# Turning the solved blocks behind the second gap's mixture pieces, from the sixth unit on

## The chip, the cores and the metric

The kernel runs on one core of one Trainium2 chip. The core has a matrix engine (TensorE, "PE" in the profile, with its weight loads as "PEld"), three engines for elementwise work (VectorE "DVE", ScalarE "ACT", GpSimd "POOL"), a queue that issues transfers (SyncE "SP"), the on-chip memory SBUF and the accumulators of TensorE, PSUM. The metric is the time on the device in microseconds (us), the median of the runs of a version.

## The reference

Two blocks follow each other. The first is a recurrence over 768 time steps for 4 batches of 8 heads of size 40, the second a mixture of four small networks whose weights are given by normalised probabilities:

```python
# r, k, v, w, a, b: (4, 8, 768, 40)
for t in range(S):
    kt, vt, rt = (k[:, :, t], v[:, :, t], r[:, :, t])
    wt, at, bt = (w[:, :, t], a[:, :, t], b[:, :, t])
    y[:, :, t] = np.einsum('bhd,bhde->bhe', rt, state)
    Sa = np.einsum('bhde,bhe->bhd', state, at)
    state_decay = state * wt[:, :, None, :] - np.einsum('bhd,bhe->bhde', Sa, bt)
    state = state_decay + np.einsum('bhd,bhe->bhde', vt, kt)
# y as x: (3072, 320)
p = domain_probs / (domain_probs.sum(-1, keepdims=True) + 1e-09)
for e in range(4):                            # w1: (4, 320, 1024), w2: (4, 1024, 320)
    h = np.maximum(x @ w1[e], 0.0)
    out += p[:, e:e + 1] * (h @ w2[e])
```

All of it is computed in fp32.

## The kernel before

The recurrence is cut into 12 chunks of 64 steps. A **unit** is one chunk of two batches, so there are 24 units, u = 0 to 23. For a unit the kernel does the following, and each part is a generator that is run up to its next `yield` by calls of `run`:

- `within`: the parts that don't need the state (G is the running product of w, then the turned copies NT, KT, AT, RT, VT, and products of them).
- `substitute`: a triangular system of 32 x 32 blocks is solved, on GpSimd for the units that matter here, step by step into Z. It takes about 22 us.
- `merge`: the solved blocks are turned (Qc, then QTc, on VectorE), copied to QT by GpSimd, and joined to 64 x 64 blocks by products pY and pQ on TensorE.
- `step`: the state goes one chunk on.

The mixture of a chunk runs beside the recurrence of the next units. It is cut into pieces in a list `todo`: `ups` (x @ w1 into ph, clipped by ScalarE into hs), `down_1` and `down_2` (products into PSUM tiles p, which VectorE adds, scaled by the gate, to the output tile osb). `gap(n)` of the main loop takes pieces off this list.

```python
    def merge(q):                                             # first stage
        Qc = sb.tile([P, H, Q], FP32, name="Qc", tag="q", bufs=2)
        QTc = sb.tile([P, H, Q], FP32, name="QTc", tag="q", bufs=2)
        tc.keep_in_program_order(nc.vector.transpose(out=dealt(Qc[:]), in_=q.Z))            # L568
        tc.keep_in_program_order(nc.vector.transpose(
            out=QTc[:].rearrange("p h r -> p (h r)"), in_=Qc[:].rearrange("p h c -> p (h c)")))   # L570
        q.QT = QTs()
        for i in range(P // Q):
            ins = nc.gpsimd.tensor_copy(out=q.QT[quarter(i), :, quarter(i % 2)], in_=QTc[quarter(i)])  # L576
            tc.keep_in_program_order(ins)
        yield
        py = big("pY")                                        # second stage
        for h in range(H):
            for i in (1, 3):
                nc.tensor.matmul(out=py[quarter(i - 1), h * Q:(h + 1) * Q], lhsT=q.F[quarter(i), h, 0:Q],
                                 rhs=QTc[quarter(i), h, :], start=True, stop=True)          # L583
        ...   # Yq copied from pY by ScalarE; yield; pQ (L595) from Qc and Yq, copied into QT (L600)
```

```python
    def add(to, p, sc, start=False):
        if start:
            nc.vector.tensor_scalar(out=to, in0=p, scalar1=sc, scalar2=None, op0=ALU.mult)               # L750
        else:
            nc.vector.scalar_tensor_tensor(out=to, in0=p, scalar=sc, in1=to, op0=ALU.mult, op1=ALU.add)  # L752
    ...
        def products(name, *terms):
            p = ps.tile([P, len(terms) * HD], FP32, name=name, tag="mm", bufs=3)
            ...   # matmuls, L841
        def down_1(e):
            p = products("p431", ...)
            ...
            for q, o in zip(qs, osb):
                add(o[:], p[:, wide], scale(q, e), e == 0)
            for q, o, cols in zip(qs, osb, (left, right)):
                add(o[:, cols], p[:, DM:DM + HD], scale(q, e))
```

The main loop, one pass for each u from 1 on (m is `merge` of unit u + 1, w is `within` of unit u + 2, s is `step`, `early` is u < 5):

```python
        run(w_next); run(s, 1); gap(0)
        early = u < 5
        if early:
            run(s, 1)
        run(w, 1)
        run(s)
        ...   # the chunk's mixture pieces are put on the list
        run(w, 1)
        if not early:
            run(m, 1)          # first stage of merge
        gap(1)
        ...   # loads of unit u + 3
        run(w, 2)
        if early:
            run(m, 1)
        else:
            run(s_next, 1)
            run(m, 1)          # second stage: pY
        gap(2)
        ...   # rest of merge, of within and of step; substitute(u + 2); gap(3)
```

A scheduler orders the recorded instructions of each engine; those given to `keep_in_program_order` keep their place among each other.

Of the kernel before, what the change touches and what calls it, by code (L numbers as in the profile page):

```python
# [15 lines left out]
def kernel(  # L16
# [154 lines left out]
    def begin(u):  # L171
        q = Unit()
        q.u, q.c, q.bp = u, u // (B // 2), u % (B // 2)
        q.b = [2 * q.bp, 2 * q.bp + 1]
        q.start, q.end = q.c == 0, q.c == NC - 1
        q.n = {}
        units.append(q)
        return q

    def load(q, names):  # L180
        for x in names:
            q.n[x] = t = sb.tile([P, H, D], FP32, name=f"nat{x}", tag=f"nat{x}", bufs=2 if x in "WV" else 1)
            for i, bb in enumerate(q.b):
                nc.sync.dma_start(
                    out=t[i * L:(i + 1) * L], in_=srcs[x][bb, :, q.c * L:(q.c + 1) * L, :].rearrange("h t e -> t h e"),
                )

    def load_raw(q, names):


        moves = []
        for x in names:
            q.n["raw" + x] = t = raw[x]()
            heads = srcs[x].rearrange("b h t e -> (b h) t e")[q.b[0] * H:(q.b[1] + 1) * H, q.c * L:(q.c + 1) * L, :]
            heads = heads.rearrange("n (x two) e -> x n (two e)", two=2)
            for r in range(2):
                if x in "RV":

                    sets = ((slice(0, 8, 2), slice(r, 16, 4)), (slice(1, 8, 2), slice(3 - r, 16, 4)))
                else:  # L200
                    sets = ((slice(0, 8), slice(r, 16, 2)),)
                for n, hs in sets:
                    for y, w_ in enumerate((D + Q, 2 * D - Q)):
                        o = slice(64 * r + Q * y, 64 * r + Q * y + Q)
                        moves.append(lambda eng, out=t[o, n, 0:w_], in_=heads[:, hs, Q * y:Q * y + w_]: eng.dma_start(out=out, in_=in_))
        return moves
# [10 lines left out]
    def go(moves, eng=None):  # L217
        for move in moves:
            move(eng or nc.sync)
# [343 lines left out]
    def merge(q):  # L563
# [5 lines that stand above are left out]
        tc.keep_in_program_order(  # L569
            nc.vector.transpose(  # L570
                out=QTc[:].rearrange("p h r -> p (h r)"), in_=Qc[:].rearrange("p h c -> p (h c)"),
# [8 lines that stand above are left out]
        py = big("pY")  # L580
        for h in range(H):
            for i in (1, 3):
                nc.tensor.matmul(  # L583
                    out=py[quarter(i - 1), h * Q:(h + 1) * Q], lhsT=q.F[quarter(i), h, 0:Q],
                    rhs=QTc[quarter(i), h, :], start=True, stop=True,
                )
        Y = sb.tile([P, H, Q], FP32, name="Yq")
        for i in (0, 2):
            nc.scalar.copy(out=Y[quarter(i)].rearrange("p h t -> p (h t)"), in_=py[quarter(i), 0:H * Q])
        yield  # L590

        pq = big("pQ")
        for h in range(H):
            for i in (0, 2):
                nc.tensor.matmul(  # L595
                    out=pq[quarter(i), h * Q:(h + 1) * Q], lhsT=Qc[quarter(i), h, :],
                    rhs=Y[quarter(i), h, :], start=True, stop=True,
                )
        for i in (0, 2):
            nc.scalar.copy(out=q.QT[quarter(i), :, quarter(1)], in_=by(pq[quarter(i), 0:H * Q], Q))  # L600
        yield
# [160 lines left out]
    def mixture_of_unit(q):  # L762

        hs, at = {}, 2 * E * q.u

        def ups(e):
            hs[e] = [up(at + 2 * e + x, q.xT, P, P) for x in range(2)]
            used(at + 2 * e + 2)
            if q.u == 0 and e + 2 < E:
                load_w2(e + 2)  # L770

        def down(e):
            po = ps.tile([P, DM], FP32, name="po", tag="mm", bufs=3)
            for f in range(NF):
                nc.tensor.matmul(  # L775
                    out=po[:], lhsT=hs[e][f // HF][:, f % HF, 0:P], rhs=w2_sb[e][:, f, :],
                    start=(f == 0), stop=(f == NF - 1),
                )
            if e == 0:
                q.osb = outputs()  # L780
            add(q.osb[:], po[:], scale(q, e), e == 0)
            if e == E - 1:
                store(q, q.osb)

        todo.append(lambda: ups(0))
        for e in range(E):
            todo.append(lambda e=e: down(e))
            if e + 1 < E:
                todo.append(lambda e=e: ups(e + 1))
# [113 lines left out]
    def begin_later(n):  # L903
        for move in later[:n]:
            tc.keep_in_program_order(move(nc.sync))
        del later[:n]

    def mix(n):

        for piece in todo[:n]:  # L910
            piece()
            begin_later(3 if n > 1 else 6)
        del todo[:n]

    def run(gen, n=99):
        if gen is None:
            return
        for _ in range(n):
            if next(gen, gen) is gen:
                break  # L920
# [3 lines left out]
    def begin_step(u):  # L924
        q = units[u]
        if q.bp == 0:
            chunks_x[q.c] = sb.tile([P, 3, 2 * P], FP32, name="xT", tag="xT", bufs=2)
        q.xT = chunks_x[q.c][:, :, q.bp * P:(q.bp + 1) * P]
        return step(q, q.xT)
# [91 lines left out]
    for u in range(1, NU):  # L1021
        q = units[u]
        m = s_next = w = w_next = iter(())
        if u + 1 < NU:
            m, s_next = merge(units[u + 1]), begin_step(u + 1)
            w_next = ws[u + 1]
        if u + 2 < NU:
            w = ws[u + 2]

        def gap(n, pieces=None):  # L1030
            at = 4 * u + n
            run(sum_ops, sums_at.get(at, 0))
            mix((1 if at in sparse else 2) if pieces is None else pieces)

        run(w_next)
        run(s, 1)
        gap(0)
# [7 lines that stand above are left out]
        if u == 1:  # L1045
            mixture_of_unit(q)
        elif q.bp:
            mixture_of_chunk(units[u - 1:u + 1], chunks_x[q.c])
        begin_later(len(later))
        run(w, 1)  # L1050
        if not early:
            run(m, 1)
        gap(1)

        if u + 3 < NU:
            go(load_raw(begin(u + 3), "WA"))
            load(units[u + 3], "WBKV")
            later.extend(load_raw(units[u + 3], "VR"))
# [13 lines that stand above are left out]
        if u + 2 < NU:  # L1072
            substitute(units[u + 2], nc.gpsimd)
        run(w, 1)
        if u + 3 < NU:
            ws.append(within(units[u + 3]))
            run(ws[u + 3], 1)
# [3 lines that stand above are left out]
            run(m)  # L1081
            gap(3, 1)
            run(s_next, 1)
            mix(0 if 4 * u + 3 in sparse else 1)
        else:
            gap(3)
        s = s_next
# [31 lines left out]
```

## Time and profile before

Three runs of the kernel took 1149.42, 1144.72 and 1143.64 us, so the median is 1144.72 us. The profiled execution spans 1139.1 us.

| from the page | value |
|---|---|
| TensorE busy | 1099.4 us |
| VectorE busy | 757.8 us |
| GpSimd busy | 473.6 us |
| ScalarE busy | 338.0 us |
| Qc, QTc on VectorE | 24 each, median 628 and 403 ns |
| QT copies on GpSimd (L576) | 96, mean 537 ns |
| pY matmuls (L583) | 768, in 24 groups of 32 |
| transfers | 122.16 MB, mean 107 GB/s |

How to read it: a group of instructions has a line of the kernel ("L568"), an engine, an operation and its tiles, written as out<-in. "Idle before" is time for which the engine stood still just before these instructions, with what released it. The answer on waits says who waited for whom: the sum in us, how many times, and the longest. A timeline lists an engine's instructions in order of time; neighbours of one kind are merged with their count, and a bracket gives the idle time ahead of them. Listed durations of neighbours overlap[...], so that the distance from start to start is what an instruction costs in a row. A TensorE that is listed as busy is not thereby at its peak.

### The profile page before, as it was taken

How to read it: one execution, taken by the hardware profiler on the slowest of the kernel's cores; microseconds unless marked ns; L12 is line 12 of the kernel's file. 1: busy time of each engine (PE TensorE's matmuls, PEld its weight loads, DVE VectorE, ACT ScalarE, POOL GpSimd, SP SyncE). 2: the span in 40 equal slices, each digit the busy share in tenths (PEclk: the TensorE clock that was granted, in tenths of full speed). 3: DMA queues.
4: the chain of work that ended last, by engine and by line, in shares of the span. 5: the costliest groups of instructions: out<-in, count | busy, mean ns of one | idle time of the engine just before them, and what ended most of it. 6: DMA issues, size and time to landing. Idle time of an engine off the chain costs nothing.

```text
span 1139.1 us, 38245 instructions
## 1 busy us (share of the span) xinstructions
PE 1099.4 (97%) x16036; PEld 976.6 (86%) x16036; DVE 757.8 (67%) x1553; ACT 338.0 (30%) x860; POOL 473.6 (42%) x1221
## 2 busy tenths in 40 slices
PE   6899997999999999999999999999999999999998
PEld 5777776888998989889899898888989898888887
DVE  8756647697767768667677677677677586553343
ACT  2333333333233232332332332332332322311110
POOL 4005626662724635625526526437337246340000
PEclk8899998999999999999999999999999999999999
DMA  7784643254263454444453453443543442231330
GB/s 118 213 245 124 131 99 78 65 132 101 76 146 89 107 128 100 119 122 101 115 121 83 123 118 86 118 102 84 139 102 87 117 110 64 75 90 55 105 92 12
DMA packets 268867, 122.16 MB, mean 107 GB/s; under 512 B 213737, under 2 KB 242073, under 8 KB 268697
## 3 DMA queue, kind: packets, MB, share of 16 engines
q1 hardware_dynamic: 265416, 119.12, 42.7%
q8 instruction: 126, 2.06, 0.8%
q10 hardware_dynamic: 3280, 0.61, 0.3%
q14 instruction: 45, 0.36, 0.1%
HBM read 111.79 MB, written 3.93 MB: 102 GB/s over the span
## 4 chain that ended last, share of the span: by engine, by line
PE 87%; DVE 4%; SPq 2%; DMA 2%; POOL 2%; ACT 2%; issue 1%; DVEq 0%; ACTq 0%
PE ph L734 29%; PE p L841 28%; PE ph L726 9%; PE pdy L371 4%; PE pfe L371 2%; PE psat L371 2%; PE pxr L371 2%; PE prn L371 2%; PE po L775 2%; PE pQ L595 1%; PE pc L371 1%; PE pY L583 1%; PE pev L371 1%; POOL Z L557 1%; PE pg L335 1%
## 5 line engine op out<-in xcount | busy, mean ns | idle before, releaser
L734 PE MATMUL ph<-xT,w1p 128*128 128x256 f32 (+1 forms) x1520 | 344.1, 379 | 2.2 <-issue 2.2
L734 PEld LDWEIGHTS ph<-xT,w1p 128*128 128x128 f32 x1520 | 274.3, 190 | 65.1 <-issue 27.3
L544 POOL TENSOR_TENSOR Z<-M,Z 128x62 f32<-128x62 f32 (+7 forms) x352 | 143.3, 407 | 368.6 <-DVE M L535 336.0
L557 POOL TENSOR_TENSOR Z<-Z 128x31 f32<-128x31 f32 (+7 forms) x704 | 257.2, 365 | 55.2
L835 DVE TENSOR_TENSOR a<-hs 128x512 f32<-128x512 f32 x220 | 152.4, 710 | 128.2 <-ACT hs L739 128.2
L739 ACT ACTIVATE hs<-ph 128x512 f32<-128x512 f32 (+1 forms) x208 | 115.7, 564 | 295.5 <-PE ph L734 295.1
L841 PE MATMUL p<-sums,a 128*128 128x160 f32 x1056 | 165.1, 299 | 0.0
L752 DVE SCALAR_TENSOR_TENSOR osb<-p,gate,osb 128x320 f32<-128x320 f32 (+1 forms) x243 | 107.9, 481 | 74.9 <-PE p L841 70.9
L841 PEld LDWEIGHTS p<-sums,a 128*128 128x128 f32 x1056 | 152.9, 190 | 2.3
L726 PE MATMUL ph<-xT,w1p 64*128 64x256 f32 (+1 forms) x760 | 110.1, 398 | 1.2 <-issue 1.1
L841 PE MATMUL p<-w,hs 128*128 128x160 f32 x704 | 102.9, 299 | 0.0
L841 PE MATMUL p<-w,a 128*128 128x160 f32 x704 | 102.8, 299 | 0.0
L841 PEld LDWEIGHTS p<-w,hs 128*128 128x128 f32 x704 | 100.3, 190 | 2.2
L841 PEld LDWEIGHTS p<-w,a 128*128 128x128 f32 x704 | 98.0, 190 | 0.0
L576 POOL COPY QT<-QTc 32x256 f32<-32x256 f32 x96 | 51.6, 537 | 111.5 <-DVE QTc L570 103.7
L726 PEld LDWEIGHTS ph<-xT,w1p 64*128 64x128 f32 x760 | 67.8, 187 | 14.4 <-issue 4.4
L519 DVE STREAM_TRANSPOSE M<-blocks 128x1024 f32<-128x1024 f32 x24 | 47.0, 1957 | 23.1 <-ACT blocks L516 23.0
L414 DVE RECIPROCAL gp<-gp 128x320 f32<-128x320 f32 x24 | 51.7, 2152 | 0.8
L504 ACT COPY EV<-pev 64x160 f32<-64x160 f32 x96 | 23.4, 286 | 66.8 <-PE pev L371 66.3
L371 PE MATMUL pdy<-VC,k_tok 64*64 64x104 f32 (+1 forms) x768 | 41.6, 260 | 0.1
L600 ACT COPY QT<-pQ 32x256 f32<-32x256 f32 x48 | 17.4, 362 | 79.3 <-PE pQ L595 78.8
L626 ACT COPY SN<-prn 128x256 f32<-128x256 f32 x44 | 15.7, 370 | 84.1 <-DVE RH L621 81.9
(148 smaller groups left out, 1364.0 us busy)
## 6 DMA issues: line engine op xcount, KB each, us to landing
w1p<-in_moe_w_dram SPq DMA_DIRECT2D x95, 512.0 KB
w1p<-in_moe_w_dram SPq DMA_DIRECT2D x190, 64.0 KB
w<-in_moe_w_dram SPq DMA_DIRECT2D x4, 1280.0 KB
sums<-in_moe_w_dram SPq DMA_DIRECT2D x9, 512.0 KB
natW<-in_w_dram SPq DMA_DIRECT2D x48, 80.0 KB
natB<-in_b_dram SPq DMA_DIRECT2D x48, 80.0 KB
natK<-in_k_dram SPq DMA_DIRECT2D x48, 80.0 KB
out_dram<-osb SPq DMA_DIRECT2D x46, 80.0 KB
```

The source lines that it names most:

```text
L371: nc.tensor.matmul(out=p[row][half(col), lo + at * out_cols:lo + (at + 1) * out_cols], lhsT=lhsT, rhs=rhs, start=(n == 0), stop=(n == len( ...
L414: pin(nc.vector.reciprocal(out=gp[:], in_=gp[:]))
L519: ins = nc.vector.transpose(out=M[:], in_=cols)
L544: ins = eng.tensor_tensor(out=Z[:, 1:3, 0:n, j + 1:Q], in0=M[:, j:j + 2, None, j + 1:Q].to_broadcast([P, 2, n, m]), in1=Z[:, here, 0:n, j: ...
L557: eng.tensor_tensor(out=z[:, 0], in0=z[:, 0], in1=z[:, x], op=ALU.add)
L576: ins = nc.gpsimd.tensor_copy(out=q.QT[quarter(i), :, quarter(i % 2)], in_=QTc[quarter(i)])
L726: nc.tensor.matmul(out=ph[i][:, f, :], lhsT=w1.last[i * DT:(i + 1) * DT, f, :], rhs=xT[i * DT:(i + 1) * DT, 2, :], start=(f == 0), stop=False,
L734: nc.tensor.matmul(out=ph[i][:, f, :], lhsT=w1.main[:, g, at * P:(at + 1) * P], rhs=xT[:, g, :], start=False, stop=(g == 1 and f == HF // ...
L739: nc.scalar.activation(out=h[:, i * HF // 2:(i + 1) * HF // 2, 0:n], in_=ph[i][:], func=ACTF.Relu,)
L752: nc.vector.scalar_tensor_tensor(out=to, in0=p, scalar=sc, in1=to, op0=ALU.mult, op1=ALU.add)
L835: nc.vector.tensor_tensor(out=t[:], in0=x, in1=y, op=op)
L841: nc.tensor.matmul(out=p[:, n * HD:(n + 1) * HD], lhsT=a[:, f, :], rhs=b[:, f, :], start=(f == 0), stop=(f == HF - 1),)
```

## The change

In the passes u = 5 to 22 the first stage of `merge`, which is the two transposes on VectorE and the four copies on GpSimd, is recorded behind the mixture pieces of the second gap, `gap(1)`, where it was recorded ahead of them. Qc needs Z, which GpSimd is still solving; the purpose is that VectorE shouldn't hold the mixture's adds back while it waits for Z. The number of instructions stays the same.

```diff
@@ main loop
         begin_later(len(later))
         run(w, 1)
+        gap(1)
         if not early:
             run(m, 1)
-        gap(1)
 
         if u + 3 < NU:
             go(load_raw(begin(u + 3), "WA"))
```

## The prediction

> **What bounds the kernel now.** I read the page's busy shares first, then its 40 slices, then the waits of the steady stretch, and last the timelines of VectorE and TensorE around one of the moved instructions.
>
> The page's first part (busy us, share of the span, instructions):
> ```profile
> PE 1099.4 (97%) x16036; PEld 976.6 (86%) x16036; DVE 757.8 (67%) x1553; ACT 338.0 (30%) x860; POOL 473.6 (42%) x1221
> ```
> TensorE is in work for 1099.4 of 1139.1 us; VectorE has a third of the span free. The answer for the stretch 240 to 1020 us, in which all of the change lies, is sharper: of 780.00 us TensorE is busy 774.90, at a granted clock of 1.00. The waits of TensorE in that stretch (us in total, times, longest) are all there is to win:
> ```profile
> PE psat L371 <- issue: 2.5, 2, 1.5
> PE pdy L371 <- DVE SX L382: 1.1, 1, 1.1
> PE ph L734 <- issue: 1.1, 1, 1.1
> PE ph L726 <- issue: 0.3, 1, 0.3
> ```
> 5.0 us, and none of it names a mixture buffer (osb, p) or the turned blocks. The waits of VectorE there show what the change is after:
> ```profile
> DVE osb L752 <- PE p L841: 32.1, 20, 3.2
> DVE Qc L568 <- POOL Z L557: 31.6, 17, 4.7
> ```
> Seventeen times VectorE stands still at the turning of the solved block (Qc), because GpSimd hasn't finished the solve (Z), and the mixture's adds (osb) queue behind it. Timeline of VectorE in the middle of the kernel (start us, us, engine, line, operation, tiles, count, idle before):
> ```profile
> 613.07 0.70 DVE L223 STREAM_TRANSPOSE RT<-rawR 128x512 f32<-128x512 f32 x1
> 615.19 0.63 DVE L568 STREAM_TRANSPOSE Qc<-Z 128x256 f32<-128x256 f32 x1 [1.42 <-POOL Z L557]
> 615.67 0.41 DVE L223 STREAM_TRANSPOSE G<-rawW 128x256 f32<-128x256 f32 x1
> 616.00 0.40 DVE L570 STREAM_TRANSPOSE QTc<-Qc 128x256 f32<-128x256 f32 x1
> 616.32 0.40 DVE L223 STREAM_TRANSPOSE G<-rawW 128x256 f32<-128x256 f32 x1
> ...
> 617.12 1.32 DVE L401 TENSOR_TENSOR_SCAN G<-G,first 128x512 f32<-128x512 f32 x1
> 618.47 0.18 DVE L405 TENSOR_TENSOR gl<-gl,G 128x8 f32<-128x8 f32 x1
> 618.58 1.58 DVE L752 SCALAR_TENSOR_TENSOR osb<-p,gate,osb 128x320 f32<-128x320 f32 x4
> 620.08 0.76 DVE L382 COPY_PREDICATED VC<-mask_up,pc 128x256 f32<-128x256 int32 x2
> ```
> and of TensorE at the same place:
> ```profile
> 614.68 1.25 PE L841 MATMUL p<-sums,a 128*128 128x160 f32 x8
> ...
> 617.69 0.67 PE L371 MATMUL prn<-ident,state 64*64 64x64 f32 x32
> 618.29 0.69 PE L583 MATMUL pY<-QTc,F 32*32 32x32 f32 x32
> 618.91 1.13 PE L726 MATMUL ph<-xT,w1p 64*128 64x256 f32 x8
> ```
> The reader is to see two distances. QTc ends at 616.40 and its first user on TensorE, pY, starts at 618.29: 1.9 us to spare. And TensorE runs without a hole through both, so VectorE's 1.42 us of idling costs nothing.
>
> [...] behind the waiting Qc nothing ran for 1.42 us. So both what the change lets go first and what it puts last follow from queue order. [...] behind the 4.86 us hole at 187 us the 32 pY matmuls took 1.07 us, elsewhere 0.69, also behind the 0.65 us hole at 229 us. [...] while the a sums (two inputs in SBUF) ran at 602 to 606 us, two pairs of GpSimd adds took 1.40 and 1.57 us, pairs of about that size before them 0.72 to 0.77.
>
> **The change part by part.** Nothing is added or removed. The first stage of merge, which is Qc and QTc on VectorE and four QT copies on GpSimd, is recorded behind the second gap instead of ahead of it, in the 18 passes u = 5 to 22. The built program shows where it lands. TensorE, GpSimd and the DMA queue keep their order; ScalarE in most passes lets the first Yq copy go ahead of the first SN copy; VectorE changes in every one of the 18. In 13 passes (u = 8 to 20) the order was RT, Qc, G, QTc, G, gl, memset, scan, gl, four osb adds, VC, VC; it becomes RT, G, G, gl, memset, scan, gl, four osb adds, Qc, VC, QTc, VC. In the other five there is no G block here (u = 5 to 7, 21, 22; at u = 22 RH stands where VC does, at u = 5 two weight sums stand ahead of the adds).
>
> What it takes away: the wait for Z, 31.6 us of VectorE. By then Z is done (615.15 in the piece above). VectorE isn't the bound and no TensorE wait is for the adds, so I count zero.
>
> What it puts in: QTc later, with pY at the same place in TensorE's queue. The program has pY wait for exactly QTc. I lay the new order out with start-to-start steps from the timeline above:
> - G block after RT. Before, the first G to the adds took 618.58 − 615.67 = 2.91 us, less the QTc between (0.32): 2.59 us, beginning about 0.07 before RT's listed end of 613.77. Adds at 616.29. Their p ended at 615.93, so they don't wait.
> - four adds: 620.08 − 618.58 = 1.50. Qc at 617.79.
> - Qc to the next instruction: 0.48 to 0.50. One VC: 0.38. QTc: 0.40 to its end. Release of pY after QTc's end: 0.06 (hole at 229 us: QTc ended at 229.97, pY began at 230.02).
> - sum: pY can begin at RT's end + 5.36 = 619.13, against 618.29 now. The 1.9 us to spare become a hole of **0.84 us**.
>
> The same sum for every pass from the timelines. With the G block, u = 8 to 20, RT end + 5.36 less pY's start: 0.99, 0.92, 0.81, 0.84, 0.81, 0.84, 0.81, 0.85, 0.82, 0.85, 0.81, 0.73, 0.82, together 10.9 us. Without it the adds begin when p ends, so pY can begin at p's end + 0.04 + 1.50 + 0.50 + 0.38 + 0.40 + 0.06 = p's end + 2.88. For u = 5, 6, 7 and 21 p ended 2.36 us ahead of pY: a hole of 0.52 each, 2.1 us. At u = 22 there is less between p and pY (1010.25 and 1011.28): 1.85 us. Total 10.9 + 2.1 + 1.85 = **14.8 us**.
>
> All of it lies on the path that sets the end. TensorE has no later wait that could swallow a delay (5.0 us in 780), and the work that feeds the next pass hangs on TensorE: VectorE's a sums wait for hs, hs for ph. A pass simply becomes longer by its hole.
>
> One term comes on top. The G block moves into the last 1.4 us of the solve, which VectorE slept through before; its gl and scan have two inputs in SBUF and meet GpSimd's adds of 0.23 to 0.31 us. I take half of one, 0.13 us, 13 times: 1.7 us. This is an estimate from those durations. The sum is 16.5 us; 1144.7 + 16.5 = **1161 us**, 1.4% more.
>
> **The rivals.**
> (a) The adds were the hidden brake: freeing p and osb 2 us sooner lets the mixture's matmuls run on, and the time falls. For it: the 31.6 us at Qc is the largest avoidable wait of VectorE. Against it: TensorE never waits for osb or p in the stretch, and the next product (p75, 623.54) starts 3.5 us after the adds are done. At best it takes back some of the 5.0 us: 1140 us.
> (b) The delay is hidden, because pY has slack or because a later wait absorbs it: 1145 us. Against it: the slack is 1.9 us and the move is 2.7 us (616.40 to 619.07), with 0.06 us of release; u = 7 had only 0.22 us of slack, and the adds alone take 1.5. For it: my steps are read from overlapping records, good to perhaps 0.1 us each.
> (c) The holes are larger. QT's copies on GpSimd also start 2.7 us later, and psat needs them; before they ended at 619.08, psat began at 629.58, so 10 us cover it. New osb tiles wait for the stores of the last chunk: at the pass of 575 us the stores were issued by 564.3 and the add would now want the tile at about 572.7, 8 us later. If either failed, or a hole came to 1.5 us, the sum would be 27 us: 1172.
> (d) The scan and the GpSimd adds block each other for whole instructions, and Z ends past 617.8, so that Qc waits again. It would have to lose 2.6 us; one scan is 1.32. That adds perhaps 0.3 us a pass: 1166.
>
> **Range and chances.** The direction rests on one subtraction made 18 times with the same sign. An error of 0.3 us a pass is 5 us, and the times before scatter from 1143.6 to 1149.4. So 1153 to 1168 should hold it 8 times in 10. Two per cent is 22.9 us, or 1167.6: that needs holes of 1.27 us on average, as in (c). Faster by 2% would need 22.9 us out of a 5.0 us stock.
>
> **What will show it.** If I am right: TensorE's list of waits gains a row pY, waiting for QTc, of about 15 us in 17 or 18 times, the longest near 1.9 at the last pass; the row Qc, waiting for Z, all but vanishes; the pass grows from 43.5 us (one pY at 574.74, the next at 618.29) to about 44.4; the clock stays 1.00; busy times of all engines stay as they are. Wrong if pY shows no such wait (then b), if TensorE waits for osb or for QT from GpSimd (c), or if Qc still waits for Z (d).

## The result and the profile after

| | before | changed |
|---|---|---|
| median of the runs made together | 1145.34 us | 1158.08 us |
| ratio | | 1.0109 (95%: 1.0075 to 1.0142) |
| profiled span | 1139.1 us | 1155.3 us |

The kernel became 12.7 us slower. 1161 was predicted.

The page's first part shows that the work is the same: TensorE is busy for 3.8 us more over a span that is 16.2 us longer, and VectorE, the engine that the change meant to relieve, for 0.2 us less. Some 1.5 us of the 16.2 lie ahead of the first changed pass, where the two programs are the same: without its new hole pY would begin there at 269.22 us, against 267.67 before. In the first 100 us of these two executions TensorE's granted clock was 0.88, against 0.91.
```profile
PE 1103.2 (95%) x16036; PEld 979.6 (85%) x16036; DVE 757.6 (66%) x1553; ACT 341.3 (30%) x860; POOL 471.9 (41%) x1221
```
The waits of TensorE from 240 to 1040 us, which hold the same 18 passes (us in total, times, longest), have a new first row; the others stood there before:
```profile
PE pY L583 <- DVE QTc L570: 14.4, 18, 0.9
PE psat L371 <- issue: 2.5, 2, 1.4
PE pdy L371 <- DVE SX L382: 1.1, 1, 1.1
PE ph L726 <- issue: 0.3, 1, 0.3
```
In the waits of VectorE of that stretch the row of Qc has all but gone, from 31.6 us to
```profile
DVE Qc L568 <- POOL Z L557: 0.2, 1, 0.2
```
So VectorE got what it was to get, and TensorE pays. In the pass that the prediction laid out, the timeline of VectorE (start us, us, engine, line, operation, tiles, count) has no wait from 621 to 628 us, and the moved pair stands behind the adds:
```profile
621.68 0.70 DVE L223 STREAM_TRANSPOSE RT<-rawR 128x512 f32<-128x512 f32 x1
622.31 0.88 DVE L223 STREAM_TRANSPOSE G<-rawW 128x256 f32<-128x256 f32 x2
...
624.97 1.59 DVE L752 SCALAR_TENSOR_TENSOR osb<-p,gate,osb 128x320 f32<-128x320 f32 x4
626.48 0.61 DVE L568 STREAM_TRANSPOSE Qc<-Z 128x256 f32<-128x256 f32 x1
626.94 0.44 DVE L382 COPY_PREDICATED VC<-mask_up,pc 128x256 f32<-128x256 int32 x1
627.27 0.42 DVE L570 STREAM_TRANSPOSE QTc<-Qc 128x256 f32<-128x256 f32 x1
```
and TensorE at the same place:
```profile
627.84 0.69 PE L583 MATMUL pY<-QTc,F 32*32 32x32 f32 x32 [0.91 <-DVE QTc L570]
```
QTc ends at 627.69, pY starts at 627.84, and in front of it stands a hole of 0.91 us where the kernel before had none. Behind it pY takes its usual 0.69 us.

### The profile page after: what moved, and what is told of

Same layout as the page of the kernel before. It is cut to its first block, busy times and chain, and to the rows that moved or that the text cites. A ratio compares the mean times of both kernels' runs of the same rounds, so it can differ in the third digit from the quotient of the medians.

```text
span 1155.3 us, 38242 instructions
## 1 busy us (share of the span) xinstructions
PE 1103.2 (95%) x16036; PEld 979.6 (85%) x16036; DVE 757.6 (66%) x1553; ACT 341.3 (30%) x860; POOL 471.9 (41%) x1221
## 4 chain that ended last, share of the span: by engine, by line
PE 68%; DVE 17%; SPq 4%; POOL 3%; issue 3%; DMA 3%; ACT 2%; DVEq 0%; ACTq 0%; POOLq 0%
PE ph L734 24%; PE p L841 22%; PE ph L726 7%; DVE osb L752 3%; POOL Z L557 2%; PE pfe L371 2%; PE psat L371 2%; PE pxr L371 2%; SPq L711 2%; PE pdy L371 2%; PE po L775 2%; DVE gp L414 1%; DVE G L401 1%; SPq L205 1%; DVE a L835 1%
## 5 line engine op out<-in xcount | busy, mean ns | idle before, releaser
L576 POOL COPY QT<-QTc 32x256 f32<-32x256 f32 x96 | 46.9, 488 | 154.8 <-DVE QTc L570 151.0
L371 PE MATMUL pdy<-SX,n_tok 64*64 64x104 f32 (+1 forms) x768 | 38.9, 247 | 1.1 <-DVE SX L382 1.1
```

What stands on the lines that cost most here:

```text
L371: nc.tensor.matmul(out=p[row][half(col), lo + at * out_cols:lo + (at + 1) * out_cols], lhsT=lhsT, rhs=rhs, start=(n == 0), stop=(n == len( ...
```

## The experiments

The theory was that TensorE sets the time, that pY's wait for the later QTc is the whole loss, and that VectorE's wait for Z, which the change removed, had been free. The rivals were that the new order on VectorE costs by itself, that a microsecond of VectorE in front of the adds counts as such, and that earlier adds do win something that the holes hide. The ratios below are to the kernel before, in runs on the same chip.

### The changed kernel, with pY one mixture piece later

In the 18 passes, gap(2)'s two pieces are split and pY is recorded between them. The last argument, 3, keeps the number of transfers that each piece issues; the lines that hand it on are left out here.
```diff
         if early:
             run(m, 1)
+            gap(2)
         else:
             run(s_next, 1)
+            gap(2, 1, 3)
             run(m, 1)
-        gap(2)
+            mix(1, 3)
```


> The changed kernel with the second stage of merge (pY) moved behind the first mixture piece of the third gap, in the same 18 passes: on TensorE, 24 matmuls of ph (4.6 us from the first to the next product in the trace before) now stand between prn and pY; the order on VectorE and GpSimd stays that of the changed kernel. Theory (the loss is pY waiting for the later QTc, and nothing else): all holes close, the wait of pY for QTc goes from 14.4 us to below 1, and the time comes back to that of the kernel before, 1143 to 1147 us. Rival 1 (the order on VectorE itself costs: adds behind the running product, QT and RH later): stays near 1158. Rival 2 (the adds' release was worth something, hidden by the holes): below 1140.

Measured: 1148.4 us, ratio 1.0027 (1.0014 to 1.0040), profiled span 1143.6 us. The row of pY is gone from TensorE's waits (240 to 1040 us), and what is left is the stock that the kernel before had, too:
```profile
PE psat L371 <- issue: 2.8, 3, 1.5
PE ph L726 <- issue: 1.3, 2, 1.0
PE pdy L371 <- DVE SX L382: 1.0, 1, 1.0
```
The late Qc and QTc are still there, and of the loss 3 us are left. So the order on VectorE by itself doesn't make the loss, and the earlier adds win nothing that shows. The time lies just above the expected 1143 to 1147, so the next run asks whose the 3 us are.

### The control: the kernel before, with pY one piece later

The same edit of pY, with Qc and QTc ahead of the adds as they were.

> The kernel before with only the other edit: pY behind the first mixture piece of the third gap, Qc and QTc where they were. It is the control for the run that put this edit on the changed kernel and came 0.27% above the kernel before. Theory (the placing of Qc costs nothing once pY stands later; the remainder comes with the move of pY): 1146 to 1149, the same as that run. Rival (the remainder is a cost of the late Qc): 1144 to 1146, the same as the kernel before.

Measured: 1147.17 us, ratio 1.0031 (1.0019 to 1.0042). It is the same as the run above, so the remainder belongs to pY's move. Side by side the four kernels are two by two: with pY early, the place of Qc makes 1.0109; with pY late, it makes no difference that shows (1.0027 against 1.0031, good to some 2 us). The timeline of TensorE shows where the 3 us arise, here in the pass u = 13, which lies at 618 us in the kernel before:
```profile
622.56 0.67 PE L371 MATMUL prn<-ident,state 64*64 64x64 f32 x32
...
633.04 0.69 PE L595 MATMUL pQ<-Yq,Qc 32*32 32x32 f32 x32
```
From the start of these prn matmuls to the start of pQ it is 10.48 us. In the kernel before it is 10.29, from 617.69 to
```profile
627.98 0.69 PE L595 MATMUL pQ<-Yq,Qc 32*32 32x32 f32 x32
```
The matmuls between are the same and TensorE has no hole, but their order differs. Half of the difference is that the first eight product matmuls take 1.19 us to the next group where they follow pY's small tiles, and 1.08 us where they follow ph's large ones. The stretch is about 0.2 us longer in each of the 18 passes, in this run and in the one above: 3.6 us.

### The kernel before, without the wait for Z

```diff
-                for x in range(1, 3):
+                for x in range(1, 2 if q.u >= 6 else 3):
                     eng.tensor_tensor(out=z[:, 0], in0=z[:, 0], in1=z[:, x], op=ALU.add)
```
This leaves out the second of the two adds of each step of the solve, from unit 6 on; its time is of a kernel with less work on GpSimd.

> The kernel before with a shortened solve on GpSimd for units 6 on: the second of the two adds of each of the 16 steps is left out, so the solved blocks lack those terms; some 16 times 0.36 us = 5.8 us less per unit; all queue orders stay. Z is then done before VectorE comes to Qc, so the 31.6 us that VectorE waits for Z, which the change was made to remove, go away without anything being moved. Theory (that wait is free, TensorE sets the time): the row Qc waiting for Z vanishes, the time stays within 1140 to 1146, the few passes with little slack at pY having no holes to lose. Rival (freeing the adds earlier is worth something): down by up to 20 us, about 1125.

Measured: 1144.83 us, ratio 0.9993 (0.9979 to 1.0007). Waits of VectorE, 240 to 1020 us:
```profile
DVE a L835 <- ACT hs L739: 112.2, 32, 5.4
DVE osb L752 <- PE p L841: 40.1, 33, 3.1
```
Qc isn't among them any more. The row of the adds, 32.1 us before, is 40.1: VectorE comes to the adds sooner and waits there for TensorE's p instead. The 31.6 us that the change was after were worth nothing that this measurement, good to 0.14% or 1.6 us, can see.

### More work on VectorE, where there is slack and where there is none

Qc is transposed three times, which writes the same values again. One run puts this into the kernel before, one into the changed kernel.
```diff
-        tc.keep_in_program_order(nc.vector.transpose(out=dealt(Qc[:]), in_=q.Z))
+        for _ in range(3 if q.u >= 6 else 1):
+            tc.keep_in_program_order(nc.vector.transpose(out=dealt(Qc[:]), in_=q.Z))
```


> The kernel before with Qc transposed three times instead of once, for units 6 on (the same result written again): two more VectorE instructions of 0.63 us in 18 passes, QTc about 1.3 to 1.6 us later, the order of all other engines unchanged. Theory (QTc's lateness counts only beyond the slack that pY has): 13 passes have 1.9 us of slack and pay nothing, the few with 0.2 to 1.5 us pay together some 3 us: 1147 to 1150. Rival (a microsecond of VectorE ahead of the adds costs as such): 18 times 1.3, so about 1168.

Measured: 1147.66 us, ratio 1.0015 (1.0003 to 1.0028). TensorE's wait in 240 to 1040 us (lines below the edit move by one):
```profile
PE pY L584 <- DVE QTc L571: 2.0, 3, 1.4
```
Three passes pay, u = 6, 7 and 22, and the others nothing: 36 more VectorE instructions for 2 us. In the kernel before, pY began 1.12, 0.22 and 1.25 us after QTc's end in these three, and about 1.9 us or more after it in 13 others. (At u = 8, with 0.62 us, nothing was lost, as VectorE waits there for Z for 1.43 us in this trace and 2.54 in the other.) Lateness counts only beyond pY's slack.

> The changed kernel with Qc transposed three times, for units 6 on: the same two more instructions as in the other run, but where no slack is left. With a VC and an AT instruction between them, QTc comes about 1.9 us later; the scheduler answers by putting half of the first ph matmuls (0.5 us) ahead of pY. Theory: each hole grows by about 1.4 us, 18 times, to some 2.3: pY waits for QTc about 40 us in all, time about 1182 (1176 to 1188). Rival (holes are absorbed, or the loss has another cause): about 1158 to 1162.

Measured: 1205.9 us, ratio 1.0535 (1.0505 to 1.0566). The direction is that of the theory; the size isn't. Waits of TensorE, 240 to 1090 us:
```profile
PE pY L584 <- DVE QTc L571: 32.4, 18, 2.1
```
The wait grew by 18.0 us, to less than the 40 us expected, and the time by 47.8, to more than the 1182 us expected. The timeline of TensorE at one of the holes shows where more went:
```profile
650.20 0.69 PE L584 MATMUL pY<-QTc,F 32*32 32x32 f32 x32 [2.07 <-DVE QTc L571]
...
651.46 5.41 PE L735 MATMUL ph<-xT,w1p 128*128 128x256 f32 x16
```
Sixteen matmuls that take 3.72 us elsewhere take 5.41. The answer for the stretches around it (us from start, length, TensorE busy and its instructions, granted clock, share and rate of the transfers) names the reason:
```profile
648.00:651.00 3.00, 0.93 (x36) 1.00 0.08 18
651.00:654.00 3.00, 3.00 (x12) 0.69 0.78 226
654.00:657.00 3.00, 3.00 (x13) 0.74 0.64 111
```
The granted clock is 0.69 and 0.74 in the two stretches behind the hole and 1.00 in those around them, which comes to 3.4 us at half rate. In 13 of the 18 passes the stretch from pY to the next product is 1.6 to 3.1 us longer than in its quick neighbours. The holes of the changed kernel, 0.48 to 0.95 us, do this in none of its 18 passes: from 240 to 1040 us its granted clock is 1.00. That called for a run between the two.

### The changed kernel, with Qc transposed twice

> The changed kernel with Qc transposed twice, for units 6 on: QTc 0.78 us later (one Qc and one VC step), pY where it was. Each hole grows from 0.9 to about 1.7 us. If only the holes count: 18 times 0.78, so 1172. If holes of this size also halve the granted clock, as 12 to 13 of 18 holes of 1.3 to 2.1 us did in the run with three transposes, for 3.4 us each at a loss of about 1.65 us: 20 us more, so about 1192, and the clock record of the profile shows stretches at half speed behind pY.

Measured: 1185.96 us, ratio 1.0373 (1.0343 to 1.0404), that is 42.8 us above the kernel before, between the two expected figures. Waits of TensorE, 240 to 1090 us:
```profile
PE pY L584 <- DVE QTc L571: 27.7, 18, 1.8
```
The holes are 27.7 us. In 8 of the 18 passes the stretch from pY to the next product took longer than its usual 5.25 us: 6.9 us in seven and 8.5 in one, together 14.8 us more. The sum is 42.5. So both parts are needed, and with both the account closes. Behind five holes of 1.22 to 1.25 us and five of about 1.65 us the stretch kept its length, while behind eight of 1.62 to 1.79 us it didn't; with three transposes it was longer behind two of the first three holes of 1.3 us, too.

Here are two holes of this run that are nearly equal, one of 1.62 us (639.43 to 641.05) and one of 1.64 us (686.38 to 688.02, of which 1.05 us lie in the first line behind the dots). A line is one stretch (from:to, length, TensorE busy and its instructions, granted clock, share and rate of the transfers):
```profile
639.18:642.60 3.42, 1.80 (x59) 1.00 0.06 13
642.60:646.01 3.41, 3.41 (x10) 0.50 0.66 202
...
686.97:690.38 3.41, 2.36 (x43) 1.00 0.25 73
690.38:693.79 3.41, 3.41 (x19) 1.00 0.70 192
```
Behind the first the granted clock is 0.50 for 3.41 us, behind the second it stays at 1.00. So in this run the length of a hole doesn't tell by itself whether it costs clock. What does was not shown: no run moved a hole of the same length to another time.

One stretch of TensorE holds nearly all that these runs changed: from the start of the prn matmuls ahead of pY to the start of pQ, added up over the 18 passes, 185.2 us in the kernel before. In the table each stretch is of one execution, and the medians are of all runs of a kernel.

| kernel | waits of pY | stretch longer by | median longer by |
|---|---|---|---|
| before, without the wait for Z | 0 | 0.0 us | -0.8 us |
| before, Qc three times | 2.0 us | 3.9 us | 2.1 us |
| before, pY later | 0 | 3.6 us | 4.0 us |
| changed, pY later | 0 | 3.6 us | 2.8 us |
| changed | 14.4 us | 16.3 us | 12.7 us |
| changed, Qc twice | 27.7 us | 43.8 us | 42.8 us |
| changed, Qc three times | 32.4 us | 62.4 us | 60.3 us |

What the stretch has above the waits is, as far as the timelines show it, the half clock where Qc is transposed more than once, the order of TensorE's matmuls around pY, and 0.05 to 0.07 us at most holes that the listed idle time leaves out.

### The rule used on a real hole

In the kernel before, pY waits for QTc at u = 3 for 4.86 us and at u = 4 for 0.65 us. There the last gap's mixture piece goes ahead of pY.
```diff
         if early:
+            if u >= 3:
+                gap(3, 1)
             run(m, 1)
             run(s_next, 1)
             run(m)
-            gap(3, 1)
+            if u < 3:
+                gap(3, 1)
+            elif u == 4:
+                mix(1)
             run(s_next, 1)
-            mix(0 if 4 * u + 3 in sparse else 1)
```


> The kernel before with the same rule used where TensorE does wait for QTc: in the passes u = 3 and 4 the mixture piece of the last gap goes ahead of pY instead of behind pQ (the fifth pass has a second piece, which stays between pQ and psat). In the trace before pY waited 4.86 us at u = 3 and 0.65 us at u = 4. Theory: these 5.5 us go, and about 1 us comes back where nothing stands between pQ and psat at u = 3: 1141, 0.4% less. Rival (the chain through GpSimd's solve sets these passes, so the hole only moves on): 1145.

Measured: 1146.25 us, ratio 1.0040 (1.0025 to 1.0055), slower by 0.4%. The profiled execution took 1151.58 us, at the upper end of the scatter. Two waits of TensorE from 0 to 260 us in the kernel before,
```profile
PE pY L583 <- DVE QTc L570: 6.5, 3, 4.9
PE psat L371 <- DVE RH L621: 1.4, 1, 1.4
```
and in this one:
```profile
PE psat L371 <- DVE RH L621: 9.5, 2, 8.0
PE pY L583 <- DVE QTc L570: 1.0, 1, 1.0
```
pY's wait shrank, and the next member of the chain, psat, now waits 8.0 us for RH at u = 3. The time behaved as the rival said, but its reason, GpSimd's solve, isn't what the trace shows. RH adds prn to EV. EV's last copy ends at 178.44 us and the prn matmuls end at 199.61; VectorE has no idle time from 196 us on, and comes to RH 8.2 us after prn's end, behind the a sums and other work:
```profile
205.17 2.74 DVE L835 TENSOR_TENSOR a<-hs 128x512 f32<-128x512 f32 x4
207.83 0.54 DVE L621 TENSOR_TENSOR RH<-prn,EV 128x160 f32<-128x160 f32 x2
```
In the kernel before prn ends at 194.87, and the first half of RH starts 1.1 us later, ahead of that work:
```profile
195.96 0.32 DVE L621 TENSOR_TENSOR RH<-prn,EV 128x160 f32<-128x160 f32 x1
```
So with this edit the scheduler put RH behind other work of VectorE, and the hole went where RH is used. It is the loss of this document's change once more, on another tile. Whether the rule would win with RH kept early wasn't tried. From 160 to 260 us TensorE is busy for 86.40 us at a clock of 0.91; in the kernel before it was 89.09 at 0.95. No version here beats the kernel before.

## Why the prediction was right

- **The bound.** TensorE, with 5.0 us of stock. Shown: the wait for Z can be taken away without a gain that shows (0.9993), and with pY late the place of Qc has no effect that shows.
- **The holes.** 14.8 us were worked out, the trace has 14.4. With the G block, 0.73 to 0.99 each was expected; 0.86 to 0.95 was found, for instance 0.91 where the sum of steps gave 0.84. Without it, 0.52 was expected and 0.48, 0.49 and 0.48 found, at u = 5, 6 and 21. u = 7 has 0.74, because Z ended just too late (357.01 us, and Qc starts at 357.04), which is the one wait of 0.2 us at Qc; the step that treated Z as always done failed there.
- **The release.** 0.06 us was taken from a single earlier pass. In the steady passes it is 0.15 (627.69 to 627.84). These 0.09 us account for the 0.07 by which the hole at 627 us came out longer.
- **The last pass.** 1.85 us was expected and 0.55 came. The step that failed is that TensorE's order stays: at u = 22 the scheduler put six of the eight first ph matmuls ahead of pY, and they fill part of the hole. The split isn't free: from prn to pQ this pass takes 11.53 us, against 10.29 before, so it lost 1.24 us and not 0.55.
- **VectorE beside GpSimd.** 1.7 us were added for the two engines delaying each other, which was the author's estimate. The step from the first G to the adds was worked out as 2.59 us and is 2.66 in the trace, so 0.07 where 0.13 was allowed; GpSimd's last adds of the solve show no delay (0.52 us for the last pair, 0.51 before). Without this term and with 0.55 at the last pass the sum would be 13.5; the longer releases and u = 7 bring it to the 14.4 of the trace. So errors of both signs are behind the close hit of 1161 on 1158. The 12.7 us between the medians have an interval of 8.6 to 16.3 (0.75% to 1.42% of 1145 us), which holds the 14.4 and just holds the 16.3 of the whole stretch.
- **Nothing swallowed the delay.** The middle pass was to grow from 43.5 us to about 44.4; most of these passes measure 44.5.
- **Rival (c)** was rightly held unlikely: no wait of TensorE from 240 to 1040 us names QT or osb. But its sum was wrong. It put 27 us on holes of 1.5 us. The run whose holes come to 27.7 us cost 42.8, as the longer stretches behind the holes add 14.8. The prediction that the clock stays at 1.00 held for the changed kernel, with its holes of up to 0.95 us; with Qc transposed more often it was 0.50 for 3.41 us behind a hole of 1.62 us, and 0.69 and 0.74 behind one of 2.07 us.

## What to carry to other kernels

Where one engine has hardly a hole, as TensorE here with 5.0 us in 780, don't count an idle time elsewhere as a gain unless it shows up as a wait of that engine: 31.6 us of VectorE's waits were worth nothing measurable. Before moving work off a "wait", look up how much slack the moved result's first user on the busy engine has. Lay out the new queue order with start-to-start steps, and compare it with that user: here this gave the hole to within 0.16 us in 16 of 18 passes, before any run. Let the user move along with what it uses: with pY one piece later, the change costs nothing that shows over that same move without it. Check afterwards that the scheduler hasn't put another result of the chain behind other work, as it did with RH.

## What the runs showed of the hardware that was not expected

TensorE's granted clock fell behind single holes of pY. With Qc transposed twice, the matmuls behind the hole took longer in 8 of 18 passes with holes of 1.2 to 1.8 us, and with three transposes in 13 of 18 with holes of 1.3 to 2.1 us. In the pass shown above the clock was 0.50 for 3.41 us, from 642.60 to 646.01. In seven of the 8 passes this cost about 1.65 us of matmul time (6.9 us for 5.25), about as much again as the hole itself, and in one 3.25 us (8.5 for 5.25). Behind the holes of the changed kernel, 0.48 to 0.95 us, the clock stayed at 1.00 in all 18 passes. Of the two holes of 1.62 and 1.64 us shown above, one was followed by a clock of 0.50 and the other by 1.00; why was not shown. The cost of a wait on TensorE was therefore not linear in its length here.
